# Folding two head pairs of batch 1 as q, then k, in one-bank tiles, with the last 64 queries' scores as a group of their own

## The chip, the core and the metric

The kernel runs on one core of a Trainium2 chip. The metric is the device time of one execution in microseconds (us). The kernel before takes 300.17 us, the median of three runs (299.82 to 300.18).

The engines are named as the profile names them: PE is TensorE's matmuls, PEld its weight loads, DVE is VectorE, ACT is ScalarE, POOL is GpSimd, SP is SyncE, which here only issues transfers. Each engine works through its own list of instructions in the written order and waits, at an instruction, for the results that it needs from others.

## The reference

Causal attention with a window of 64 over 8 batches, 8 heads, 576 positions and head size 64, followed by a two-layer network on all 4608 tokens with the gate h * relu6(h + 3) / 6 between the layers:

```
scores = (q @ k.transpose) / sqrt(64)
rel = pos[:, None] - pos[None, :]
scores = where((rel >= 0) & (rel < 64), scores, -1e9)
attn_out = softmax(scores) @ v                       # (8, 8, 576, 64)
x = attn_out.transpose(0, 2, 1, 3).reshape(4608, 512)
h = x @ w_in                                         # w_in: 512 x 2048
out = (h * clip(h + 3, 0, 6) / 6) @ w_out            # w_out: 2048 x 512
```

## The kernel before, in words

**Two interleaved halves.** The network is cut into nine tiles of 512 tokens. For tile t the hidden layer H(t, fc) is made for 16 blocks fc of 128 features (`s1_part`, L737): four matmuls each, one for each pair of heads, since a pair's two heads of 64 make 128 input rows. ScalarE and VectorE apply the gate (L750, L755) and write `gT`. Then the output rows Y(u) of four blocks of 128 tokens are made (`s2_part`, L776), 16 matmuls each in parts of four, copied out of PSUM (L789) and stored by SP. Batch t + 1's attention is put into the gaps of tile t, for tile t + 1 needs its result. Tile 1 reads the last rows of batch 0 and most of batch 1.

**Attention of one batch.** The eight heads are handled as four pairs, 0 to 3. For each pair there are: the transposed q and k; the scores (L581) of eight blocks of 64 queries with the two blocks of keys that each can see; the exponential (L597, ScalarE) and the multiplication with a mask of zeros and ones (L606, VectorE), which give `pT`; the sums with the values V. The ninth block of 64 queries of all four pairs forms an item of its own, "e", with its own tile `p9`.

**What is special in batch 1.** Its q and k are not turned by a transfer but loaded with nine tokens to a partition into `Aq` and `Ak`, two pairs to a load, and transposed by TensorE (`fold_four`, L540): 36 small transposes for q and 36 for k of two pairs, into one two-bank tile of PSUM each. One copy of 1152 columns for q and one for k (L545) then bring them to `Fq` and `Fk`. The weighted sums of the pairs give rows of queries (`pv_rows`, L626), which VectorE divides by their sums (L636 reciprocal, L637 product); the quotient is transposed back on TensorE (`turn_x`, L652) and copied to `xT` (L368). Only e goes the other way (`pv`, L678): its sums come out transposed already, and the division is made by a logarithm (L684) and an exponential (L687) on ScalarE and a product (L698) on VectorE. All later batches use `pv` for everything.

**V.** Values land as blocks of 128 tokens. Every second block of queries needs keys shifted by 64 tokens, so each pair of heads has two shifted copies of V (`shift_v`, L456): one of 512 elements on 64 partitions and one of 384. A pair's sums need both. For batch 1 each copy may be made by POOL, ACT or DVE, and all need the values landed. In the program before, pair 0's two are made by DVE and ACT, pair 1's by DVE, pairs 2's and 3's by POOL.

**PSUM.** Eight banks: two single ones (`pn`) for the network, and three tiles of two banks, `pb` and two `pa`, which the attention and the hidden layer share.

**What sets the order.** Nothing runs when it can: a planner (`Plan.solve`) gives each operation a cost in ns and places them one by one; for operations with alternatives it picks the engine that would end first by its costs; landing times of POOL's loads are a written list (`NEXT`) with a margin of 300 ns. The order that it finds is then written out, engine by engine, and is fixed. So an edit in one place can change the engine of a copy, the bank of a result and the order of later work. `gate = (hs[4],)` lets batch 1's folds start once H(0, 4) has been placed; which part of the output they stand between, and what comes between two of them, is the planner's doing.

The lines that the change touches, and what leads to them:

Of the kernel before, what the change touches and what calls it, by code (L numbers as in the profile page):

```python
# [222 lines left out]
def kernel(  # L223
# [302 lines left out]
    def fold_four(g0, b, gate, kinds=("b", "a")):  # L526

        pair = slice(g0, g0 + 2)
        names = {n: ("F", n, b, g0) for n in "qk"}
        op = pe(2 * R * 33 + 30, None, [("A", n, g) for n in "qk" for g in (g0, g0 + 1)] + ["fold"], [("ps", x) for x in names.values()],  # L530
                "pick", alloc=tuple(names.values()), kinds=kinds, after=gate, mode="r")

        def em():
            for n, x in names.items():
                to = wide(op, x).bitcast(BF16)
                for j in range(R):
                    for g in (g0, g0 + 1):
                        for h in range(2):
                            r, o = (slice(y * D, (y + 1) * D) for y in (h, home(b, g, h)))
                            nc.tensor.transpose(out=to[o, g - g0, j * D : (j + 1) * D], in_=A[n][r, g, j, :], identity=fold[r, :])  # L540

        op.emit = em

        def ev(eng, n, x):
            cpy(eng)(out=F_[n][:, pair, :].rearrange("d g (p j) -> d g p j", j=R),  # L545
                     in_=wide(op, x).bitcast(BF16)[:, :, 0:S].rearrange("d g (j p) -> d g p j", p=D))

        for n, x in names.items():
            alts = {e: (c, (lambda e=e, n=n, x=x: ev(e, n, x)), False) for e, c in (("DVE", dve(2 * S)), ("ACT", act(2 * S)))}
            e = add("DVE", 0, None, reads=[("ps", x)], writes=[t_key(n, b, g) for g in (g0, g0 + 1)], alts=alts, stream="copy", prio=300)  # L550
            e.frees = (x,)
        return op

    def scores(b, items, gate, stream="att", pr=300, masked=False, kinds=("a",)):

        names = tuple(("S", b, x) for x in items)
# [237 lines left out]

    def attend(b, first, second, stream="att", rows=()):
        a, i0 = scores(b, (0, 1), first, stream)
        z, i1 = scores(b, ("e", 2, 3), second + (a,), stream, kinds=("b", "a"))
        todo = list(zip((0, 1, "e", 2, 3), (*i0, None, *i1)))
        if rows:
            todo.append(todo.pop(2))  # L800
        for x, i in todo:
            if x in rows:
                _, *og = pv_rows(b, x, i, (z,), stream)
                turn_x(b, x, *og, stream, kinds=("b", "a"))
            else:
                pv(b, x, i, (z,), stream)
# [109 lines left out]
    for t in range(NTT):  # L916
        head = HEAD if len(x_parts(t)[1]) == 1 else 0
        if t == 0:
            head = HEAD0
            for gs, n in ((range(2), head), (range(2, NG - 1), SOON)):  # L920
                for fc in range(n):
                    s1_part(t, fc, gs)
        else:
            for fc in range(head):
                s1_part(t, fc, range(NG - 1))

        def seen(t, fc, head):
            return 0 if fc >= head else 2 if t == 0 and fc >= SOON else NG - 1

        hs = [s1_finish(t, fc, s1_part(t, fc, range(seen(t, fc, head), NG))) for fc in range(NFC)]  # L930
        ys = {}
        us = range(4 * t, 4 * t + 4)
        if t == 0:
            for pair in (us[:2], us[2:]):
                for part in (range(0, NFC // 2), range(NFC // 2, 3 * NFC // 4), range(3 * NFC // 4, NFC)):
                    for u in pair:
                        ys[u] = s2_part(u, part)
                for u in pair:
                    s2_close(u, ys[u][-1])
        else:  # L940
            for u in us:
                for cols in (((0, DM),) if u < NT // P - 1 else ((0, 3 * P), (3 * P, DM))):
                    s2_close(u, s2_part(u, range(NFC), cols=cols)[-1], cols)
        b = t + 1
        if b < B:
            if b == 1:
                gate = (hs[4],)
                cast_v(iv, 0, 2, (THREE,) * 3, parts=REST, prio=-2500, pieces=(1,))
                scores(0, ("e",), gate, "pick", kinds=("b", "a"))
                pv(0, "e", None, (), "pick")  # L950
                then(load_vrows(1, NE, chain))
                for g in range(0, NG, 2):
                    fold_four(g, 1, gate)
                for g in range(NG):
                    shift_v(g, g + 1, THREE)
                attend(1, gate, gate, "pick", ROWS)
            else:
                for g in range(0, NG, 2):
                    shift_v(g, g + 2, ("ACT", "DVE") if b == 2 else ("DVE",))
                attend(b, (hs[LATE if b > ROWS_FROM else -1],), (hs[-1],))  # L960
            if b + 1 < B:
                load_rows(b + 1)
# [53 lines left out]
```

## Time and profile before

| | |
|---|---|
| median of three runs | 300.17 us |
| the profiled execution | 299.94 us |
| its span, first to last instruction | 298.2 us |
| granted TensorE clock | 0.999 |
| PE busy | 287.2 us, 96% |
| ACT busy | 206.5 us, 69% |
| DVE busy | 199.8 us, 67% |
| POOL busy | 121.9 us, 41% |
| output matmuls (L776), bank pn, 128x512 | 533 recorded, 124.9 us |
| fold of q, then k, of pairs 2 and 3 | starts at 41.17 and 41.48 us |
| hidden layer of tile 1 | starts at 52.12 us |
| hidden layer of tile 2 | starts at 83.68 us |

A row of the profile in order of time has the start, the duration, the engine, the line of the kernel, the operation, what it writes and reads, the shapes and how many instructions were merged; in brackets is how long the engine stood idle before it and what ended that. Matmuls are pipelined: the next row may start before the one above has ended, and a single record may be missing. A row of grouped instructions ends with the busy time, the mean time of one in ns, and the idle time ahead of them. For transfers, "DMA to landing" counts from the start of the issuing instruction.

### The profile page before, as it was taken

Reading aid. Unit: us, or ns where it says so; the run is one execution under the profiler, and the core shown is the slowest. Engines: PE = TensorE matmul, PEld = TensorE weight load, DVE = VectorE, ACT = ScalarE, POOL = GpSimd, SP = SyncE. Lnnn points to the kernel's source line nnn. Section 1 sums busy time; section 2 is a strip of 40 time slices with the busy share of each in tenths; the row PEclk is TensorE's granted clock in tenths of the full one; section 3 lists DMA queues with packets and bytes.
Section 4 is the critical chain, followed back from the end, with each engine's and each line's share of the span. In section 5 each row is a group of like instructions: output and inputs, shape, how many; then the busy total and the mean of one; then the engine's idle time right before and its main releaser. Section 6 shows DMA issues by size and latency. Waiting matters only on the chain.

```text
span 298.2 us, 6926 instructions
## 1 busy us (share of the span) xinstructions
PE 287.2 (96%) x2780; PEld 153.4 (51%) x2825; DVE 199.8 (67%) x327; ACT 206.5 (69%) x319; POOL 121.9 (41%) x170
## 2 busy tenths in 40 slices
PE   6899998999999999999999999999999999999996
PEld 6544555445544554455687554455445544444443
DVE  4768639777777975878678767878677868106700
ACT  3878636887968795778687958886787768227611
POOL 8884667069547916930992069405000000000000
PEclk9999999999999999999999999999999999999999
DMA  8999999999999999989996899969900110110011
GB/s 187 189 207 206 203 191 176 191 95 151 132 201 150 117 151 196 169 55 209 142 165 40 139 184 171 68 118 167 116 2 35 37 70 1 37 70 35 0 73 70
DMA packets 137680, 36.66 MB, mean 123 GB/s; under 512 B 126256, under 2 KB 132912, under 8 KB 137648
## 3 DMA queue, kind: packets, MB, share of 16 engines
q0 software_dynamic: 98816, 17.80, 73.9%
q1 hardware_dynamic: 38688, 18.12, 25.2%
q8 instruction: 22, 0.36, 0.5%
q10 hardware_dynamic: 144, 0.29, 0.4%
q14 instruction: 10, 0.08, 0.1%
HBM read 36.70 MB, written 9.44 MB: 155 GB/s over the span
## 4 chain that ended last, share of the span: by engine, by line
PE 81%; DMA 10%; POOL 3%; issue 3%; DVE 2%; ACT 0%; POOLq 0%; DVEq 0%
PE pn L776 36%; PE pn L737 16%; PE pa L737 12%; PE pb L737 9%; DMA Aq<-in_q_dram 4%; DMA V<-in_v_dram 4%; PE pa L678 4%; DMA Ak<-in_k_dram 2%; PE pa L581 2%; PE pa L776 1%; PE pb L678 1%; DVE opg L637 1%; DVE pT L606 1%; POOL V L389 0%; POOL Aq L389 0%
## 5 line engine op out<-in xcount | busy, mean ns | idle before, releaser
L776 PE MATMUL pn<-wout,gT 128*128 128x512 bf16 x533 | 124.9, 379 | 2.1 <-issue 1.1
L737 PEld LDWEIGHTS <-win 128*128 128x128 bf16 x640 | 62.0, 98 | 60.5
L776 PEld LDWEIGHTS <-gT 128*128 128x128 bf16 x592 | 54.5, 98 | 58.0 <-issue 0.2
L737 PE MATMUL pn<-xT,win 128*128 128x512 bf16 (+1 forms) x270 | 61.1, 357 | 0.3
L750 ACT ACTIVATE t<-pn,half 128x512 bf16<-128x512 f32 x62 | 42.6, 689 | 8.7 <-PE pn L737 8.3
L755 DVE SCALAR_TENSOR_TENSOR gT<-t,pa 128x512 bf16<-128x512 bf16 x47 | 32.2, 687 | 24.2 <-ACT t L750 23.9
L737 PE MATMUL pa<-xT,win 128*128 128x512 bf16 (+1 forms) x202 | 48.0, 358 | 0.4
L755 DVE SCALAR_TENSOR_TENSOR gT<-t,pn 128x512 bf16<-128x512 bf16 x62 | 42.5, 686 | 8.4 <-ACT t L750 8.1
L389 POOL DMA_DIRECT2D nk<-in_k_dram x55 | 42.0, 797 | 4.8 <-DMA Tk<-nk 4.1
L389 POOL DMA_DIRECT2D V<-in_v_dram x40 | 33.2, 848 | 14.4 <-PE pa L678 12.0
L750 ACT ACTIVATE t<-pa,half 128x512 bf16<-128x512 f32 x47 | 32.2, 686 | 8.9 <-PE pa L737 8.5
L698 DVE TENSOR_TENSOR xT<-pa,rec 64x512 bf16<-64x512 f32 (+1 forms) x48 | 32.0, 667 | 9.3 <-ACT rec L687 8.4
L737 PE MATMUL pb<-xT,win 128*128 128x512 bf16 (+1 forms) x153 | 36.3, 357 | 0.5 <-issue 0.5
L755 DVE SCALAR_TENSOR_TENSOR gT<-t,pb 128x512 bf16<-128x512 bf16 x35 | 24.0, 686 | 16.2 <-ACT t L750 16.1
L789 ACT COPY osb<-pn 128x512 f32<-128x512 f32 x18 | 10.5, 585 | 33.1 <-PE pn L776 33.1
L684 ACT ACTIVATE rec<-pa 64x512 f32<-64x512 f32 (+1 forms) x48 | 27.6, 574 | 5.1 <-PE pa L678 4.0
L750 ACT ACTIVATE t<-pb,half 128x512 bf16<-128x512 f32 x35 | 24.2, 690 | 7.6 <-PE pb L737 7.5
L389 POOL DMA_DIRECT2D nq<-in_q_dram x30 | 27.0, 900 | 3.2 <-DMA wout<-in_moe_w_out_dram 1.6
L597 ACT ACTIVATE pT<-pa 128x1024 bf16<-128x1024 f32 x25 | 24.6, 1021 | 1.0 <-PE pa L581 0.9
L606 DVE TENSOR_TENSOR pT<-pT,mask 128x1024 bf16<-128x1024 bf16 x28 | 19.2, 704 | 3.7 <-ACT pT L597 3.6
L678 PEld LDWEIGHTS <-V 128*128 128x128 bf16 x448 | 16.8, 98 | 6.7 <-DVE xT L698 0.8
L854 POOL COPY scrap<-Tq 128x1 bf16<-128x1 bf16 x5 | 0.9, 189 | 45.3 <-DMA Tq<-nq 45.3
(93 smaller groups left out, 203.9 us busy)
## 6 DMA issues: line engine op xcount, KB each, us to landing
out_dram<-osb SPq DMA_DIRECT2D x35, 256.0 KB, 3.1
V<-in_v_dram POOLq DMA_DIRECT2D x28, 128.0 KB, 5.7
nq<-in_q_dram POOLq DMA_DIRECT2D x24, 128.0 KB, 4.7
nk<-in_k_dram POOLq DMA_DIRECT2D x41, 64.0 KB, 4.0
wout<-in_moe_w_out_dram POOLq DMA_DIRECT2D x4, 512.0 KB, 14.5
win<-in_moe_w_in_dram POOLq DMA_DIRECT2D x3, 512.0 KB, 9.3
V<-in_v_dram POOLq DMA_DIRECT2D x12, 64.0 KB, 6.0
Aq<-in_q_dram POOLq DMA_DIRECT2D x2, 288.0 KB, 13.7
```

What stands on the lines that cost most here:

```text
L389: em = lambda: e.dma_start(out=out_ap, in_=in_ap)
L581: nc.tensor.matmul(to[o, home(b, g, h) if x == "e" else h, y * D : (y + 1) * D], lhsT=w, rhs=q_cols(b, r, g, j), start=not masked, stop=no ...
L597: nc.scalar.activation(out=p_[:].rearrange("p j h c -> p h j c"), in_=wide(add_far if masked else op, name)[:, :, 0 : n * D].rearrange("p ...
L606: nc.vector.tensor_tensor(out=pp, in0=pp, in1=mask[:, m0 : m0 + n, :, :].rearrange("p j h c -> p (j h c)"), op=MULT)
L678: nc.tensor.matmul(wide(op, name)[:, h, y * D : (y + 1) * D], lhsT=V[:, blk, g, h * D : h * D + P], rhs=p_[:, y, home(b, g, h) if end else ...
L684: add("ACT", act(n), lambda h=h: nc.scalar.activation(out=rc[rows[h], 0:n], in_=wide(op, name)[rows[1 - h], h, 0:n], func=LN), reads=[key] ...
L698: nc.vector.tensor_tensor(out=o, in0=a, in1=z, op=MULT)
L737: nc.tensor.matmul(bank(op, name)[:, to : to + n], lhsT=win16[:, g, fc * P : (fc + 1) * P], rhs=xT[:, g, o : o + n], start=(g == 0), stop= ...
L750: nc.scalar.activation(out=t1[ti][:], in_=bank(op, name), func=RELU, bias=half[:], scale=1.0 / 6.0)
L755: nc.vector.scalar_tensor_tensor(out=gT[:, fc, :], in0=t1[ti][:], scalar=1.0, in1=bank(op, name), op0=MIN, op1=MULT)
L776: nc.tensor.matmul(bank(op, name)[:, 0:n], lhsT=gT[:, fc, col : col + P], rhs=wout16[:, fc, js], start=(fc == 0), stop=(fc == NFC - 1))
L789: alts = {e: (f(n), (lambda e=e: cpy(e)(out=osb[oi][:, js], in_=bank(op, name)[:, 0:n])), False) for e, f in (("DVE", dve), ("ACT", act))}
```

## The change: two folds in place of one, and e after pairs 2 and 3

For pairs 2 and 3 of batch 1 `fold_four` is replaced by two calls of a new function `fold_two`, one for q and one for k. Each makes the same 36 transposes, but a pair's go to a tile of its own (one bank of it is used), and each pair has a copy of its own of 576 columns, for which the planner picks the engine. q's fold waits only for q's load, k's only for k's. Pairs 0 and 1 stay with `fold_four`.

In `attend`, batch 1's second group of scores was e, 2, 3 in one operation. Now 2 and 3 are one operation and e another that follows it. No load is changed.

```diff
+    def fold_two(n, g0, b, gate, kinds=("b", "a")):
+        pair = (g0, g0 + 1)
+        names = tuple(("F", n, b, g) for g in pair)
+        op = pe(R * 38 + 30, None, [("A", n, g) for g in pair] + ["fold"], [("ps", x) for x in names], "pick",
+                alloc=names, kinds=kinds, after=gate, mode="r")
+        def em():
+            for j in range(R):
+                for g, x in zip(pair, names):
+                    to = bank(op, x).bitcast(BF16)
+                    for h in range(2):
+                        r, o = (slice(y * D, (y + 1) * D) for y in (h, home(b, g, h)))
+                        nc.tensor.transpose(out=to[o, j * D : (j + 1) * D], in_=A[n][r, g, j, :], identity=fold[r, :])
+        op.emit = em
+        def ev(eng, g, x):
+            cpy(eng)(out=F_[n][:, g, :].rearrange("d (p j) -> d p j", j=R),
+                     in_=bank(op, x).bitcast(BF16)[:, 0:S].rearrange("d (j p) -> d p j", p=D))
+        for g, x in zip(pair, names):
+            alts = {e: (c, (lambda e=e, g=g, x=x: ev(e, g, x)), False) for e, c in (("DVE", dve(S)), ("ACT", act(S) - 30))}
+            e = add("DVE", 0, None, reads=[("ps", x)], writes=[t_key(n, b, g)], alts=alts, stream="copy", prio=300)
+            e.frees = (x,)
+        return op
...
     def attend(b, first, second, stream="att", rows=()):
         a, i0 = scores(b, (0, 1), first, stream)
-        z, i1 = scores(b, ("e", 2, 3), second + (a,), stream, kinds=("b", "a"))
+        if rows:
+            z, i1 = scores(b, (2, 3), second + (a,), stream, kinds=("b", "a"))
+            z, _ = scores(b, ("e",), (z,), stream, kinds=("b", "a"))
+            i1 = (None, *i1)[1:]
+        else:
+            z, i1 = scores(b, ("e", 2, 3), second + (a,), stream, kinds=("b", "a"))
...
                 for g in range(0, NG, 2):
-                    fold_four(g, 1, gate)
+                    if g == 0:
+                        fold_four(g, 1, gate)
+                    else:
+                        for n in "qk":
+                            fold_two(n, g, 1, gate)
```

What the planner makes of it, engine by engine, from q's fold to the hidden layer of tile 1 ("4 Y" are four output matmuls; numbers are pairs):

```
PE before:  4Y 4Y 4Y 4Y 8Y  fold q,k  8Y  scores e,2,3  4Y  sums 0  4Y  sums 1  turn 0  sums 2  4Y  sums 3  turn 1  4Y  turn 2  turn 3  sums e  H
PE after:   4Y 4Y 4Y 4Y  fold q  4Y  fold k  4Y  scores 2,3  scores e  16Y  sums 0,1,2  4Y  turn 0  4Y  turn 1  sums 3  turn 2  sums e  turn 3  H
V copies before:  DVE 0,1,1   ACT 0   POOL 2,2,3,3
V copies after:   POOL 0,0,1   ACT 1,2,3   DVE 2,3
```

One tile later, in the gaps of tile 1's output, the order around batch 2's attention changes too: before, 8 Y stand between its first and second group of scores, and 4, 12, 4 and 16 between its sums and up to tile 2's hidden layer; after, 12 Y, and then 16, 4 and 12. On SP the store of row block 3 moves ahead of the transfer that turns batch 2's q. From tile 2 on the order is the same, with `pa` and `pb` in other turns.

## The prediction

> **What bounds the kernel.** I read the page first, then the instructions in order of time on TensorE, then the other engines in the same stretch.
>
> ```profile
> span 298.2 us, 6926 instructions
> ...
> PE 287.2 (96%) x2780; PEld 153.4 (51%) x2825; DVE 199.8 (67%) x327; ACT 206.5 (69%) x319; POOL 121.9 (41%) x170
> ...
> PE 81%; DMA 10%; POOL 3%; issue 3%; DVE 2%; ACT 0%; POOLq 0%; DVEq 0%
> ```
>
> TensorE is busy 96% of the span and carries 81% of the chain that ended last. A microsecond that it loses anywhere after the start is a microsecond of the total, and one it gains counts only if it is idle there now. All that changes lies between 39 and 52 us (batch 1's attention inside the second product of token tile 0), and, through the planner, in the same place one tile later (66 to 85 us). TensorE there, in order of time (start, duration):
>
> ```profile
> 35.86 5.39 PE L776 MATMUL pn<-wout,gT 128*128 128x512 bf16 x23
> 41.17 0.48 PE L540 MATMUL pb<-fold,Aq 64*64 64x64 bf16 x36
> 41.48 0.50 PE L540 MATMUL pa<-fold,Ak 64*64 64x64 bf16 x36
> 41.91 1.90 PE L776 MATMUL pn<-wout,gT 128*128 128x512 bf16 x7
> 43.74 0.29 PE L581 MATMUL pa<-Fq,Fk 64*128 64x64 bf16 x8
> ...
> 44.43 0.82 PE L776 MATMUL pn<-wout,gT 128*128 128x512 bf16 x3
> 45.71 0.45 PE L626 MATMUL pa<-V,pT 128*64 128x65 bf16 x16 [0.45 <-ACT p L597]
> ...
> 48.22 0.45 PE L626 MATMUL pa<-V,pT 128*64 128x65 bf16 x16 [0.34 <-DVE pT L606]
> ...
> 49.57 0.45 PE L626 MATMUL pa<-V,pT 128*64 128x65 bf16 x16
> 49.97 0.40 PE L652 MATMUL pb<-ident,opg 128*128 128x128 bf16 x4
> ...
> 51.65 0.40 PE L652 MATMUL pb<-ident,opg 128*128 128x128 bf16 x4 [0.19 <-DVE opg L637]
> ...
> 52.12 1.68 PE L737 MATMUL pn<-xT,win 128*128 128x512 bf16 x7
> ```
>
> The waits are 0.45, 0.34 and 0.19 us: 0.98 us is all that this stretch could give back. They come from the engines beside it:
>
> ```profile
> 44.53 0.51 ACT L456 COPY V<-V 64x384 bf16<-64x384 bf16 x1 [1.69 <-DMA V<-in_v_dram]
> 45.06 0.60 ACT L597 ACTIVATE p<-pa 128x512 bf16<-128x512 f32 x1
> ```
>
> ```profile
> 42.04 1.36 DVE L545 COPY Fk<-pa 128x1152 bf16<-128x1152 bf16 x1 [3.65 <-PE pa L540]
> 44.55 1.26 DVE L456 COPY V<-V 64x512 bf16<-64x512 bf16 x3 [1.15 <-DMA V<-in_v_dram]
> 45.85 0.74 DVE L606 TENSOR_TENSOR p<-p,mask 128x512 bf16<-128x512 bf16 x1
> ...
> 50.90 0.69 DVE L637 TENSOR_TENSOR opg<-pa,rsum 128x512 bf16<-128x512 f32 x1
> ```
>
> ```profile
> 44.86 0.91 POOL L389 DMA_DIRECT2D nq<-in_q_dram  x1
> 45.81 2.72 POOL L456 COPY V<-V 64x384 bf16<-64x384 bf16 x4
> ```
>
> Batch 1's values land at 44.5 us; eight shifted copies of V (two for each pair of heads, L456) must follow before a pair's weighted sums (L626) may start. VectorE and ScalarE take theirs the moment the values land; GpSimd takes its four only at 45.81, behind the load that it is still issuing.
>
> **The change, part by part.**
>
> *Folds earlier and split.* q's fold now stands eight output matmuls earlier, k's follows four matmuls after it. A matmul of L776 steps by 0.216 us (24 of them, one record missing, from 35.86 to 41.17 with one change of kind). So q's fold starts at 41.17 - 1.73 = 39.44, k's at 39.44 + 0.43 (41.48 to 41.91, one fold with the change back) + 0.86 + 0.10 = 40.83. Their loads:
>
> ```profile
> 24.64 0.70 POOL L389 DMA_DIRECT2D Aq<-in_q_dram  x1 [2.10 <-DMA win<-in_moe_w_in_dram]
> ...
> 27.17 0.71 POOL L389 DMA_DIRECT2D Ak<-in_k_dram  x1 [1.83 <-DMA wout<-in_moe_w_out_dram]
> ```
>
> ```profile
> DMA to landing us min/median/max: 14.4/14.4/14.4
> ```
>
> ```profile
> DMA to landing us min/median/max: 13.3/13.3/13.3
> ```
>
> q (first line) lands at 39.04, k (second) at 40.47: both just in time, by 0.4 us, so no wait; a late load costs up to 0.4. The 72 transposes stay 72. One more departure from the output matmuls and back costs 0.43 - 0.31 (41.17 to 41.48, a fold alone) = 0.12, and 0.10 to enter: +0.22 us.
>
> *Copies out of the folds.* Two of 1152 columns become four of 576:
>
> ```profile
> L518 DVE COPY Fq<-pn 128x576 bf16<-128x576 bf16 x1 | 0.8, 759 | 0.3 <-PE pn L513 0.3
> ...
> L518 ACT COPY Fk<-pn 128x576 bf16<-128x576 bf16 x2 | 1.3, 645 | 0.0
> ...
> L456 POOL COPY V<-V 64x512 bf16<-64x512 bf16 x3 | 1.9, 646 | 0.1
> L456 POOL COPY V<-V 64x384 bf16<-64x384 bf16 x3 | 1.9, 618 | 0.2
> ```
>
> 0.76 and 0.65 us, side by side. k's copy starts some 0.56 after its fold does (41.48 to 42.04), at 41.39, and ends at 42.15. TensorE has four matmuls in between and comes to the scores at 40.83 + 0.43 + 0.86 + 0.10 = 42.22: a wait of 0 to 0.1, and the scores of pairs 2 and 3 are out 1.5 us sooner than now.
>
> *Scores of the last 64 queries apart.* The same 40 score matmuls, 0.69 us (43.74 to 44.43), with e's eight at the end. Their exponential, 0.60, moves behind those of pairs 2 and 3, so the 0.45 us wait of pair 0's sums for it goes. TensorE then does 16 output matmuls, 42.95 + 3.45, and reaches pair 0's sums at 46.5.
>
> *What is late next: V's copies.* The written order gives them out anew. Because ScalarE has three exponentials and VectorE three masks from 43 to 46 us, pair 0's two copies now go to GpSimd, with one of pair 1's; ScalarE gets three (behind e's exponential), VectorE two (behind the masks). Nothing in the change makes GpSimd free sooner: the load issued at 44.86 holds it to 45.81, as now. Pair 0 is complete at 45.81 + 0.646 + 0.618 = 47.07, pair 1 at 47.69. TensorE runs in order, so pair 0's sums wait from 46.5 to about 47.15, pair 1's start at 47.77, pair 2's at 48.07 (a step of 0.3: 49.57 to 49.97 is 0.40 with a change of kind). Then 0.40 to the output matmuls, 0.96 for four with the change: first transposition 49.43; 0.24; four more; second one 50.63; pair 3's sums 50.96. Its quotient is the next wait: VectorE's reciprocal and product take 0.92 (the product at 50.90 ends at 51.59, its reciprocal began 0.23 before it), so pair 3's transposition starts at 50.96 + 0.45 + 0.92 + 0.12 for two hand-overs = 52.45, against 51.65 now, though e's sums have been moved ahead of it to fill. Hidden layer of tile 1: 52.45 + 0.24 = 52.69 against 52.12: **+0.57 us**. Unknown is what GpSimd's copies take in company; its own four here took 2.72, 0.68 each, and single ones 0.50 to 0.85. At 0.50 the term is +0.2, at 0.85 about +0.95. I take the mean of the rows. Below zero it cannot go while these copies begin at 45.81.
>
> *One tile later.* The new state of the banks lets the planner put twelve instead of eight output matmuls ahead of batch 2's second group of scores; for that only 32 instead of 36 stand between its first sums and the next hidden layer. Now:
>
> ```profile
> 73.67 0.63 PE L678 MATMUL pb<-pT,V 128*128 128x64 bf16 x16
> ...
> 79.75 0.64 PE L678 MATMUL pa<-pT,V 128*128 128x64 bf16 x16
> ...
> 83.68 0.81 PE L737 MATMUL pa<-xT,win 128*128 128x512 bf16 x3
> ...
> 84.97 0.38 PE L737 MATMUL pa<-xT,win 128*128 128x512 bf16 x1
> ```
>
> ```profile
> 74.34 1.20 ACT L684 ACTIVATE rec<-pb 64x512 f32<-64x512 f32 x2 [1.41 <-PE pb L678]
> ```
>
> ```profile
> 83.16 1.39 DVE L698 TENSOR_TENSOR xT<-pa,rec 64x512 bf16<-64x512 f32 x2
> ```
>
> From first sums to hidden layer 10.01 us, and 1.29 more to the first matmul that reads pair 3 (84.97). Pair 3's last product ends at 84.55, 10.88 after the first sums, through ScalarE's row of logarithms and exponentials that starts at 74.34. Slack 0.42. Four matmuls fewer take 0.86: the slack becomes -0.44, and a store's copy that ScalarE now does ahead of this row adds some 0.05: **+0.5 us** (0.3 to 0.6).
>
> *Queues.* GpSimd has three copies instead of four, so its later loads go out 0.6 sooner: nothing waits for them. On SP the store of row block 3 passes ahead of the transposition of q:
>
> ```profile
> 53.17 3.00 SPq L391 DMA_TRANSPOSE Tq<-nq  x1
> 56.28 0.55 SPq L389 DMA_DIRECT2D out_dram<-osb  x1
> ```
>
> Its copy is done by 51.5, so its 0.55 of issue ends before 53.17, and the transposition, which waits for its loads, stays. If it doesn't, 0.55 on a transfer whose readers start at 66 us.
>
> Sum: 0.57 + 0.5 = +1.05 us (the 0.22 for the switches is inside the first term). The profiled execution took 299.94, 0.23 below the median of 300.17; against it 301.0, as a median **301.2 us**.
>
> **Rivals.** (a) *GpSimd's copies are held up by VectorE.* Before, a mask of this shape took 0.74 beside GpSimd's first copy (45.85), and without one
>
> ```profile
> 69.55 0.43 DVE L606 TENSOR_TENSOR p<-p,mask 128x512 bf16<-128x512 bf16 x1 [0.18 <-ACT p L597]
> ```
>
> 0.43: one waits for the other. In the new order VectorE masks without a pause when GpSimd comes to its copies, the last mask about 45.7 to 46.15, so GpSimd would begin 0.34 later: +0.34 and up to 0.2 from longer copies, 301.6 us. Against it: GpSimd may come first, as before. The Trainium skill, "SBUF — State Buffer", section "Who interferes with whom", says that a VectorE instruction with two SBUF inputs and a GpSimd one that reads SBUF exclude each other for the whole instruction, and whichever starts first wins; the 0.74 against 0.43 agrees, and this rule speaks against the change. (b) *V's copies are hidden anyway:* if GpSimd is done with pairs 0 and 1 about 0.6 sooner, only the later tile's 0.5 stays: 300.6 to 300.7, no change. Against it: 45.81 depends on loads that are untouched. (c) *Faster:* the three waits go (0.98), the switch costs 0.22, and the later row of ScalarE finds its slack: 300.17 - 0.76 = 299.4. That needs pair 0's copies by 46.5, so GpSimd free by 45.2, and a row 0.5 shorter than 10.88; nothing in the profile offers either.
>
> **Chances.** Forecast 0.55 (own range 300.9 to 301.5), (a) 0.22, (b) 0.15, (c) 0.08. Within 0.2% (0.6 us), about what a measurement of this kernel can tell from no change, lies only (b); so slower 0.77, same 0.15, faster 0.08. The range 300.5 to 301.9 takes in (b), the forecast and (a) with GpSimd's copies at 0.85.
>
> **What would show it.** q's fold near 39.4, k's near 40.8 without a wait; no wait of pair 0's sums for ScalarE, but one of about 0.6 for GpSimd's V; pair 3's transposition waiting for VectorE at 52.4; hidden layer of tile 1 near 52.7; a wait of 0.5 at its pair 3 one tile later, for VectorE. I am wrong if pair 0's sums start by 46.6, if k's load is late, or if tile 2's hidden layer runs through.

## The result and the profile after

The changed kernel takes 300.88 us (median of 8 executions, 300.47 to 301.22), the kernel before 300.05 (median of 8, 299.70 to 300.63): a ratio of 1.0025, 95% interval 1.0016 to 1.0034, so 0.83 us slower. (Ratios and intervals in this document are those on record; a ratio can differ a little from the quotient of the two medians beside it.) The profiled execution of the changed kernel took 300.65 us, that of the kernel before 299.94.

From the page of the changed kernel: span, busy time by engine, the chain that ended last.

```profile
span 298.9 us, 6935 instructions
...
PE 287.8 (96%) x2780; PEld 153.7 (51%) x2825; DVE 198.4 (66%) x326; ACT 208.4 (70%) x323; POOL 120.7 (40%) x169
...
PE 86%; DVE 3%; issue 3%; POOL 3%; ACT 2%; DMA 2%; DVEq 0%; ACTq 0%; POOLq 0%
```

TensorE has 0.6 us more of busy time for the same 2780 recorded matmuls, and the span is 0.7 us longer. TensorE in order of time, in the changed stretch and then one tile later:

```profile
32.71 0.48 PE L540 MATMUL pa<-fold,Aq 64*64 64x64 bf16 x36
...
39.65 0.22 PE L567 MATMUL pb<-fold,Aq 64*64 64x64 bf16 x2
...
41.02 0.22 PE L567 MATMUL pa<-fold,Ak 64*64 64x64 bf16 x2
...
42.40 0.89 PE L608 MATMUL pa<-Fq,Fk 64*128 64x64 bf16 x32
43.13 0.28 PE L608 MATMUL pb<-Fq,Fk 64*128 64x64 bf16 x8
43.34 3.63 PE L803 MATMUL pn<-wout,gT 128*128 128x512 bf16 x15
46.90 1.16 PE L653 MATMUL pa<-V,pT 128*64 128x65 bf16 x31
...
52.10 0.40 PE L679 MATMUL pa<-ident,opg 128*128 128x128 bf16 x4 [0.41 <-DVE opg L664]
52.33 1.89 PE L764 MATMUL pn<-xT,win 128*128 128x512 bf16 x7
...
74.71 0.63 PE L705 MATMUL pb<-pT,V 128*128 128x64 bf16 x16
...
83.86 0.81 PE L764 MATMUL pa<-xT,win 128*128 128x512 bf16 x3
...
85.66 0.38 PE L764 MATMUL pa<-xT,win 128*128 128x512 bf16 x1 [0.34 <-DVE xT L725]
```

The rows at 39.65 and 41.02 are the first transposes of the two new folds. Three things are to be seen. The first row, the fold of pairs 0 and 1, is ahead of anything that the change touches, and it already stands at 32.71 against 32.47 in the trace of before. Tile 1's hidden layer (52.33) is 0.21 late against 52.12, which is no more than that. The matmul that reads pair 3 one tile later (85.66) is 0.69 late against 84.97, and has the wait of 0.34 for VectorE that was not there. So this one pair of traces puts 0.48 us (0.69 less 0.21) on the later tile and nothing on tile 1. The medians are 0.83 apart, and what lies between is what the experiments had to find.

The engines beside it, in the same two places (VectorE, GpSimd, then ScalarE and VectorE one tile later):

```profile
42.07 0.76 DVE L572 COPY Fk<-pb 128x576 bf16<-128x576 bf16 x1 [1.09 <-PE pb L567]
```

```profile
45.89 1.76 POOL L456 COPY V<-V 64x512 bf16<-64x512 bf16 x3
```

```profile
75.52 1.20 ACT L711 ACTIVATE rec<-pb 64x512 f32<-64x512 f32 x2
...
84.21 1.39 DVE L725 TENSOR_TENSOR xT<-pa,rec 64x512 bf16<-64x512 f32 x2
```

VectorE's copy of pair 3 of k begins at 42.07, though its fold was done at 41.57 (k's fold starts at 41.02): half a microsecond late, and the scores that need it stretch to 0.73 us (42.40 to 43.13). GpSimd's copies of V begin at 45.89, behind its load, and one tile later the last product ends at 85.60, with ScalarE's row starting at 75.52.

### The profile page after: what moved, and what is told of

The parts are those of the page before. It is cut to its first block, busy times and chain, and to the rows that moved or that the text cites. A ratio compares the mean times of both kernels' runs of the same rounds, so it can differ in the third digit from the quotient of the medians.

```text
span 298.9 us, 6935 instructions
## 1 busy us (share of the span) xinstructions
PE 287.8 (96%) x2780; PEld 153.7 (51%) x2825; DVE 198.4 (66%) x326; ACT 208.4 (70%) x323; POOL 120.7 (40%) x169
## 4 chain that ended last, share of the span: by engine, by line
PE 86%; DVE 3%; issue 3%; POOL 3%; ACT 2%; DMA 2%; DVEq 0%; ACTq 0%; POOLq 0%
PE pn L803 36%; PE pn L764 18%; PE pa L764 13%; PE pb L764 10%; PE pa L705 3%; PE pa L608 2%; DMA V<-in_v_dram 2%; DVE xT L725 2%; PE pa L803 1%; ACT rec L711 1%; POOL V L389 1%; DVE opg L664 1%; POOL Ak L389 1%; ACT pT L624 1%; PE pb L705 1%
## 5 line engine op out<-in xcount | busy, mean ns | idle before, releaser
L764 PE MATMUL pa<-xT,win 128*128 128x512 bf16 (+1 forms) x197 | 46.6, 357 | 0.7 <-DVE xT L725 0.3
L782 DVE SCALAR_TENSOR_TENSOR gT<-t,pa 128x512 bf16<-128x512 bf16 x46 | 31.5, 687 | 23.7 <-ACT t L777 23.4
L777 ACT ACTIVATE t<-pa,half 128x512 bf16<-128x512 f32 x46 | 31.5, 687 | 9.3 <-PE pa L764 8.8
L764 PE MATMUL pb<-xT,win 128*128 128x512 bf16 (+1 forms) x157 | 37.3, 357 | 0.5 <-issue 0.5
L782 DVE SCALAR_TENSOR_TENSOR gT<-t,pb 128x512 bf16<-128x512 bf16 x36 | 24.7, 686 | 16.3 <-ACT t L777 16.3
L777 ACT ACTIVATE t<-pb,half 128x512 bf16<-128x512 f32 x36 | 24.9, 690 | 7.7 <-PE pb L764 7.7
L624 ACT ACTIVATE pT<-pa 128x1024 bf16<-128x1024 f32 x26 | 25.6, 1021 | 1.9 <-PE pa L608 1.1
L633 DVE TENSOR_TENSOR pT<-pT,mask 128x1024 bf16<-128x1024 bf16 x28 | 18.8, 689 | 4.7 <-ACT pT L624 4.7
```

What stands on the lines that cost most here:

```text
L624: nc.scalar.activation(out=p_[:].rearrange("p j h c -> p h j c"), in_=wide(add_far if masked else op, name)[:, :, 0 : n * D].rearrange("p ...
L633: nc.vector.tensor_tensor(out=pp, in0=pp, in1=mask[:, m0 : m0 + n, :, :].rearrange("p j h c -> p (j h c)"), op=MULT)
L764: nc.tensor.matmul(bank(op, name)[:, to : to + n], lhsT=win16[:, g, fc * P : (fc + 1) * P], rhs=xT[:, g, o : o + n], start=(g == 0), stop= ...
L777: nc.scalar.activation(out=t1[ti][:], in_=bank(op, name), func=RELU, bias=half[:], scale=1.0 / 6.0)
L782: nc.vector.scalar_tensor_tensor(out=gT[:, fc, :], in0=t1[ti][:], scalar=1.0, in1=bank(op, name), op0=MIN, op1=MULT)
```

## Experiments

A table first, because one trace says little here. From trace to trace the first stage ends up to 1.5 us earlier or later: the fold of pairs 0 and 1 stands between 32.16 and 33.71 us. GpSimd's copies of V, which follow loads, begin between 45.46 and 46.09 in all of them. So tile 1's hidden layer has to be read against the fold of its own execution. The last column but one is the time from there to the hidden layer of tile 3 (two tiles on), which is 62.76 us in the kernel before. What follows, from tile 3's hidden layer to the last instruction, takes 183.33 to 183.35 us in all thirteen traces. So whatever makes one profiled execution longer than another lies ahead of tile 3: in the start of tile 1's hidden layer or in that column.

| kernel | fold | tile 1's hidden layer | from the fold to it | from it to tile 3's | median, us |
|---|---|---|---|---|---|
| before | 32.47 | 52.12 | 19.65 | 62.76 | 300.05 |
| before, more warm-up | 33.44 | 52.27 | 18.83 | 62.76 | 300.13 |
| before, twelve outputs | 33.57 | 52.35 | 18.78 | 63.26 | 300.37 |
| changed | 32.71 | 52.33 | 19.62 | 63.23 | 300.88 |
| changed, again | 33.17 | 52.31 | 19.14 | 63.21 | 300.68 |
| changed, eight outputs | 33.48 | 52.77 | 19.29 | 63.22 | 300.72 |
| the same again | 33.27 | 52.45 | 19.18 | 63.77 | 301.28 (one) |
| eight outputs, shifted | 33.48 | 52.62 | 19.14 | 63.50 | 301.13 |
| eight outputs, more warm-up | 33.71 | 52.85 | 19.14 | 63.08 | 300.88 |
| changed, VectorE's stream | 32.32 | 52.49 | 20.17 | 63.49 | 300.87 |
| changed, pair 0's values | 33.50 | 52.78 | 19.28 | 63.00 | 300.70 |
| folds alone | 32.16 | 51.86 | 19.70 | 63.62 | 300.52 |
| last scores alone | 32.73 | 52.21 | 19.48 | 62.77 | 300.68 |

Beside the changed kernel the kernel before had a median of 300.05 us; beside the changed one again, twelve outputs, eight outputs and pair 0's values also 300.05; beside the shifted one and the two single parts 300.13; beside more warm-up and VectorE's stream 299.95.

**The changed kernel again.** No edit.

> The changed kernel once more, to part what its one profiled execution cannot part. In that trace the fold of pairs 0 and 1 already stands at 32.71 us against 32.47 in the trace of before (+0.24), ahead of anything that the change touches; tile 1's hidden layer starts at 52.33 against 52.12 (+0.21, so about 0 net of that start), and one tile later the matmul of pair 3 at 85.66 against 84.97 (+0.69, so +0.46 net). Theory 1 (only the later wait costs; the early start is chance): the offset at the fold is another one here, between -0.3 and +0.3, and net of it tile 1's hidden layer again stands at 0 +-0.1 and the matmul of pair 3 at +0.45 +-0.1; medians then differ by 0.4 to 0.6 us. Theory 2 (as the prediction had it, tile 1's hidden layer is late by itself and the one trace an exception): the hidden layer net of the offset +0.4 to +0.6, medians +0.8 to +1.1. Theory 3 (the offset belongs to the changed program): the offset at the fold is +0.2 to +0.3 again, medians +0.6 to +0.8. The copy of pair 3 of k on VectorE, 0.48 us late in the first trace (start 42.07, its fold ended about 41.5): late again by 0.4 to 0.6 if it belongs to the order, under 0.1 late if it was chance.

Measured: 300.68 us, ratio 1.0019 (1.0010 to 1.0028). The fold stands at 33.17, tile 1's hidden layer at 52.31: although the stage began 0.46 us later than in the first trace, its end is at the same place. The copy on VectorE is late by half a microsecond again (42.53, its fold started at 41.48). So the offset is none of the program's (theory 3 falls), the late copy is. Theories 1 and 2 are both too simple: what the first stretch costs depends on when it begins, which the other traces settle.

**The later order alone, put into the kernel before.**

```diff
-attend(b, (hs[LATE if b > ROWS_FROM else -1],), (hs[-1],))
+attend(b, (hs[LATE if b > ROWS_FROM else -1],),
+       (hs[-1],) + ((yops[4, 8],) if b == 2 else ()))   # yops[4, 8]: the third stretch of output matmuls
```

> The kernel before with that one order put in: batch 2's second score group behind the third stretch of the output layer (12 output matmuls before it instead of 8); folds, score groups and tile 1's attention as before. Theory 1: a wait of 0.3 to 0.5 us at pair 3 of tile 2's hidden layer, that matmul 0.45 +-0.1 later than in the kernel before, and +0.35 to +0.55 us of time. Rival (the wait needs the change's own tile 1 as well, for instance the later copies of V or other buffers): no wait, time within 0.15 us of the kernel before. If the changed kernel is more than 0.2 us above this one, something else in it costs the difference.

Measured: 300.37 us, ratio 1.0011 (1.0002 to 1.0021), so +0.32. TensorE:

```profile
33.57 0.48 PE L540 MATMUL pa<-fold,Aq 64*64 64x64 bf16 x36
...
52.35 1.68 PE L737 MATMUL pn<-xT,win 128*128 128x512 bf16 x7
...
85.70 0.38 PE L737 MATMUL pa<-xT,win 128*128 128x512 bf16 x1 [0.33 <-DVE xT L698]
```

The wait is there without anything else of the change, and from tile 1's hidden layer to tile 3's it takes 63.26 us, 0.50 more than in the kernel before. Twelve output matmuls ahead of batch 2's second score group are by themselves the later wait. In time the +0.32 is a little under the +0.35 to +0.55 that was expected, with an interval of 0.06 to 0.63. The changed kernel, 300.68 on the same chip, is 0.31 above this one, more than the 0.2 that was set as the mark: something else in it costs the difference. The same rows show the other thing: in the old order a start of the stage that is 1.10 us later (33.57 against 32.47) moves the hidden layer by 0.23 only.

**That order taken out of the changed kernel.**

```diff
-attend(b, (hs[LATE if b > ROWS_FROM else -1],), (hs[-1],))
+z = attend(b, (hs[LATE if b > ROWS_FROM else -1],), (hs[-1],))
+if b == 2:
+    yops[4, 8].follows.add(z)      # second score group before the third stretch again
```

> The changed kernel with one order undone: batch 2's second score group is again ahead of the third stretch of the output layer (8 output matmuls before it as in the kernel before, not 12). Nothing in tile 1's own attention moves. Theory 1 (the later wait is the whole cost): no wait of 0.34 at pair 3 of tile 2's hidden layer, and 0.45 +-0.1 us faster than the changed kernel on the same chip, so between -0.1 and +0.15 against the kernel before. Theory 2 (tile 1's hidden layer late as well): 0.45 faster than the changed kernel, but still +0.3 to +0.6 against the kernel before. Rival: the wait at pair 3 comes from something other than the count of output matmuls (the copies of V, the loads); then the time stays within 0.15 us of the changed kernel's and the wait stays.

Measured: 300.72 us, ratio 1.0021 (1.0010 to 1.0032): nothing gained, although the wait at pair 3 is gone. TensorE stops somewhere else, inside batch 2's second group of scores:

```profile
69.30 0.63 PE L608 MATMUL pa<-Tq,Tk 64*64 64x64 bf16 x53
70.24 0.28 PE L608 MATMUL pa<-Tq,Tk 64*64 64x64 bf16 x11 [0.31 <-issue]
```

Sixty-four equal matmuls, one operation, break off after 53: from the start of one matmul to that of the next it takes 0.50 us, where the others step by 0.01, and "issue" says that the profile shows nothing that was waited for. The rival as I had put it (the wait stays) is wrong, and so is theory 1's gain.

**What that stop is.** Three more kernels with eight outputs. The first is the same program again, the next two change only how many matmuls keep TensorE busy before the first loads (41 in the others), which moves all that follows along its instruction stream.

```diff
-for _ in range(int((op.start - 350) * 0.95 / (IDLE / 1.2))):
+for _ in range(int((op.start - 350) * 0.95 / (IDLE / 1.2)) - 3):    # shifted; "+ 10" in the other
```

> The kernel with eight outputs once more, for its trace alone. If the stop of 0.50 us inside batch 2's second score group belongs to the program (to the place in the stream or to the order), it is there again, at the same matmul (54th of 64 of pairs 2 and 3). If it was chance, it is gone, and from the start of tile 1's hidden layer to that of tile 3's it takes 62.76 us as in the kernel before, not 63.22.

> The kernel with eight outputs again, with three of the matmuls left out that only keep TensorE busy before the first loads (38 instead of 41, in a stretch after which TensorE stands 0.93 us for data anyway). It moves nothing but where TensorE's instructions lie in its stream. In the run with eight outputs the wait at pair 3 was gone, but TensorE stood 0.50 us in the middle of batch 2's second score group (a weight load at 69.73, the next at 70.24) with no semaphore in between, and the time stayed at +0.67 against the kernel before. Theory A (that stop belongs to the place in the instruction stream): it is gone or elsewhere, and the time falls by 0.3 to 0.5 us against the run with eight outputs, to +0.2 to +0.4 against the kernel before. Theory B (chance of one execution): gone here too, but the time as it was, +0.55 to +0.75. Theory C (it belongs to this order of the work): there again, time +0.55 to +0.75.

> The kernel with eight outputs, with ten more of the matmuls that only keep TensorE busy before the first loads (51 instead of 41, some 0.8 us in a stretch that has 0.9 us to spare). It moves nothing but TensorE's place in its instruction stream, by 20 instructions. With eight outputs TensorE stood 0.50, 0.86 and, with seven instructions fewer, 0.60 us inside batch 2's second score group, three matmuls later for the seven instructions, and went on 1.4 to 1.5 us after a 16 KB transfer of the instruction queue ended (68.78, 68.97, 69.03 us; begun at 67.3 to 67.7, when GpSimd's loads fill the transfer engines; in the kernel before begun at 65.31, ended 66.19, and no stop). Theory D (the stop waits for that piece of the instruction stream): asked for 20 instructions earlier, the transfer begins before GpSimd's loads, at 65.5 or earlier, the stop is gone, and the time falls by 0.4 to 0.7 us against the kernels with eight outputs, to +0.15 to +0.4 against the kernel before. Theory C (the stop belongs to the order of the work): it is there, 0.5 to 0.9 us, at the same matmul, time +0.65 to +1.1.

TensorE at that place, in the run again, the shifted one, and the one with ten more:

```profile
68.98 0.63 PE L608 MATMUL pa<-Tq,Tk 64*64 64x64 bf16 x53
70.47 0.28 PE L608 MATMUL pa<-Tq,Tk 64*64 64x64 bf16 x11 [0.86 <-issue]
```

```profile
69.15 0.66 PE L608 MATMUL pa<-Tq,Tk 64*64 64x64 bf16 x56
70.40 0.26 PE L608 MATMUL pa<-Tq,Tk 64*64 64x64 bf16 x8 [0.60 <-issue]
```

```profile
69.38 0.55 PE L608 MATMUL pa<-Tq,Tk 64*64 64x64 bf16 x43
70.11 0.35 PE L608 MATMUL pa<-Tq,Tk 64*64 64x64 bf16 x21 [0.19 <-issue]
```

The same program stops at the same matmul (53 and 11). With three matmuls fewer in front it stops three later (56 and 8), with ten more ten earlier (43 and 21). So the stop belongs to a place in the instruction stream and to no piece of the work. What arrives there is seen in the transfers: the queue named "instruction" moves 16 KB at a time. In the kernel before, the one that matters lies between 65 and 66.3 us; in the run again, between 67 and 69 (packets, MB, share of 16 engines in that window):

```profile
q0 software_dynamic: 1059, 0.13, 163.1%
q8 instruction: 1, 0.02, 4.2%
```

```profile
q0 software_dynamic: 2241, 0.28, 222.1%
q8 instruction: 1, 0.02, 5.2%
```

A share of 4.2% of 16 engines over 1.3 us is 0.88 us, of 5.2% over 2 us 1.65 us. The packets of GpSimd's loads (q0) add up to 163% and 222% of the engines' time in these windows, so they overlap, and the 16 KB transfer runs beside them. Beginning, end of that transfer and the first matmul behind the stop: 67.56, 68.78, 70.24 (eight outputs); 67.32, 68.97, 70.47 (again); 67.68, 69.03, 70.40 (shifted); 66.96, 68.61, 70.11 (more warm-up); and, with the folds alone, 67.23, 68.40, 69.86. TensorE goes on 1.37 to 1.50 us after the transfer ended, in all five traces. What the stop costs is best read from the table: 0.32 to 1.01 us more than 62.76 to tile 3. In the kernel before, the transfer ended at 66.19; 1.5 us on, at 67.69, TensorE was not there yet (these 64 scores start at 68.69). In the changed kernel it ended at 68.15; 1.5 us on is 69.65, and twelve output matmuls instead of eight bring TensorE to the place 0.86 us later, at about 70.2, after that: the order with the wait at pair 3 hides the stop.

My theory D was right on what it is and wrong on the size: ten matmuls more brought the transfer forward by 0.4 to 0.7 us, not past the loads; the stop shrank to 0.4, and the time is 300.88 against 299.95 (1.0027, 1.0017 to 1.0038) instead of the +0.15 to +0.4 that I gave. The shifted kernel has 301.13 against 300.13 (1.0035, 1.0017 to 1.0052): theory A was right that the stop moves with the stream, but the time rose instead of falling to +0.2 to +0.4, for the stop only moved on. Why the transfer begins later with the two-pair folds (66.56 to 68.11 us) than with the old ones (64.92 to 66.33) isn't shown; that GpSimd's loads are in front of it is only what the shares suggest.

The same sign is to be found where the change has no part, in the first stage. In the kernel before, and in the kernel before with ten matmuls more of warm-up (tested below):

```profile
12.16 0.41 PE L513 MATMUL pn<-fold,Aq 64*64 64x64 bf16 x14 [0.19 <-issue]
```

```profile
12.15 0.26 PE L581 MATMUL pa<-Fq,Fk 64*128 64x64 bf16 x6 [0.42 <-issue]
...
18.34 0.59 PE L737 MATMUL pa<-xT,win 128*128 128x512 bf16 x2 [0.51 <-issue]
```

The first of these breaks off a group of 18 after 4, the second a group of 16 after 10, which is ten matmuls ahead in the order of work. TensorE goes on 1.40, 1.41 and 1.49 us after a 16 KB transfer ended (at 10.76, 10.74 and 16.85).

The Trainium skill, "Runtime: NRT & Kernel Launch", section "Instruction fetch mechanics", says that an engine's instructions come in blocks of 16 KiB, 256 instructions each, by a DMA queue of its own while the block before is running, and that the cost of a crossing is mostly hidden. The page of the profile of the kernel before agrees on the size for q8 (0.36 MB in 22 transfers); those of q14 are half as large:

```profile
q8 instruction: 22, 0.36, 0.5%
...
q14 instruction: 10, 0.08, 0.1%
```

Which engine a queue serves, the profile doesn't say; TensorE's 2780 matmuls and 2825 weight loads over 22 transfers are 255 instructions each, which fits q8. Most of the 22 crossings cost nothing here: in the kernel before, the 0.19 us above is the longest idle time of TensorE put down to "issue". The crossing that comes in a run of 64-column matmuls, at 0.01 us each, while GpSimd's loads are under way, costs 0.3 to 1.0 us in the five traces.

**VectorE's late copy.** The same question for the copy of pair 3 of k.

```diff
-nc.vector.memset(mask32[:], 1.0)),
+nc.vector.memset(mask32[:], 1.0),
+*(nc.vector.memset(half[:, 0:1], 0.5) for _ in range(4))),
```

> The changed kernel with four tiny fills more on VectorE in the first microsecond and a half, which move VectorE's instruction stream by four. In every run with the two-pair folds VectorE's copy of pair 3 of k starts 0.48 us after its fold is done, with no wait of its own. It is the 65th instruction of VectorE's main stream. Theory D (it waits for the next piece of VectorE's instruction stream): with four instructions more the late one is another, four instructions ahead of it; the copy starts within 0.1 us of its fold's end, the scores of pairs 2 and 3 follow without the hole of some 0.2 us, and tile 1's hidden layer starts up to 0.2 us earlier at a late start of the stage. Time 0 to 0.2 us below the changed kernel's +0.6 to +0.8. Theory E (the copy is late for what happens beside it, on ScalarE or GpSimd): late by 0.45 to 0.5 us again.

Measured: 300.87 against 299.95 us (1.0027, 1.0015 to 1.0040). VectorE and TensorE:

```profile
41.27 0.76 DVE L572 COPY Fk<-pb 128x576 bf16<-128x576 bf16 x1 [0.69 <-PE pb L567]
```

```profile
42.01 0.64 PE L608 MATMUL pa<-Fq,Fk 64*128 64x64 bf16 x32
42.49 0.28 PE L608 MATMUL pb<-Fq,Fk 64*128 64x64 bf16 x8
...
46.26 0.26 PE L653 MATMUL pa<-V,pT 128*64 128x65 bf16 x4
47.41 0.80 PE L653 MATMUL pa<-V,pT 128*64 128x65 bf16 x27 [0.89 <-POOL V L456]
```

With four instructions more in front the copy starts 0.09 us after the semaphore of its fold (41.18), and the scores take 0.48 instead of 0.73 us. So the lateness belongs to a place in VectorE's stream, as theory D had it, and theory E falls. That the copy waits for a piece of the stream to arrive isn't shown, and one thing speaks against it: in the eight other traces with two-pair folds the copy starts 0.50 to 0.51 us after its fold's semaphore, though that comes anywhere from 41.03 to 42.56 us, and the last 8 KB transfer of q14 before it ended 1.2 to 2.1 us earlier, at no fixed distance. The time, +0.92 us, didn't fall as theory D had said; what the early copy is worth at a late start this trace can't show, for its start was early. The fold stood at 32.32, the earliest but one, and what TensorE saved went into a wait of 0.89 us for GpSimd's second copy of V, which follows the loads. The 64 scores one tile later also took 1.00 us instead of 0.72, with the 16 KB transfer ending at 68.99 and TensorE going on 1.58 later: a small stop for instructions in spite of the twelve outputs, and 63.49 us to tile 3.

**Pair 0's values off GpSimd.**

```diff
-shift_v(g, g + 1, THREE)
+shift_v(g, g + 1, THREE if g else ("ACT", "DVE"), 400 if g == 0 else 0)
```

> The changed kernel with the two shift copies of pair 0's values taken from GpSimd: both are made early on VectorE (about 44.5 us), where VectorE has a hole between the masks; GpSimd keeps copies of later pairs. In the changed kernel the sums of pairs 0 and 1 stop twice for GpSimd's copies, 0.25 + 0.17 = 0.42 us. Theory 1: the sums of pair 0 do not stop, tile 1's hidden layer starts 0.2 to 0.5 us earlier than in the changed kernel (net of the start), the wait of 0.34 one tile later stays, and the time falls by 0.2 to 0.5 us against the changed kernel, to within 0.25 of the kernel before. Rival 1 (TensorE's wait moves on: turn 3 waits for VectorE's quotient in any case, 0.41 us now): hidden layer within 0.1 us of the changed kernel's, no gain, the wait at turn 3 grows to about 0.8. Rival 2 (VectorE, with two copies more, holds up GpSimd's): GpSimd's copies longer than 0.75 us, no gain or a loss.

Measured: 300.70 us, ratio 1.0024 (1.0012 to 1.0036), no gain. TensorE:

```profile
46.01 0.45 PE L653 MATMUL pa<-V,pT 128*64 128x65 bf16 x16
...
52.33 0.40 PE L679 MATMUL pa<-ident,opg 128*128 128x128 bf16 x4
52.78 0.59 PE L764 MATMUL pn<-xT,win 128*128 128x512 bf16 x2
```

Pair 0's sums run through and the last turn waits for nothing, as theory 1 had it; yet the fold is 19.28 us ahead of the hidden layer, not less than the 19.14 of the changed kernel at a like start. At such starts there was no wait for GpSimd left to remove, and what was gained at the last turn was spent ahead of the hidden layer (0.45 from the turn to it instead of 0.23). The wait one tile later is there as expected. Rival 1 is right that TensorE's wait moves on, though not on where. Rival 2 had GpSimd's copies at more than 0.75 us: the first took 0.92, the other three 0.50 to 0.59.

**Each part alone.** Folds in two, with the scores of the last 64 queries left in their group; and the reverse, with `fold_four` for all.

```diff
-z, i1 = scores(b, (2, 3), ...)            # folds alone
-z, _ = scores(b, ("e",), (z,), ...)
+z, i1 = scores(b, ("e", 2, 3), ...)
...
-for n in "qk":                            # last scores alone
-    fold_two(n, g, 1, gate)
+fold_four(g, 1, gate)
```

> One part of the change alone: pairs 2 and 3 of batch 1 folded q, then k, in one-bank tiles; the scores of the last 64 queries stay in one group with those of pairs 2 and 3. One tile later 8 output matmuls stand before the second score group, as in the kernel before. Where tile 1's hidden layer starts is told against the start of tile 0's (the first stage ends between 16.5 and 17.6 us from execution to execution): 35.62 at 16.50 and 34.75 at 17.60 in the old order, 35.59 at 16.74, 35.11 at 17.20 and 35.26 at 17.51 in the changed one. Theory 1 (at late starts the changed order of turns and sums costs 0.4 to 0.5 us because the last turn waits 0.41 us for VectorE's quotient; at early ones 0.2): this order too ends with a turn right behind its sums, so +0.2 to +0.45 us against the kernel before, and no wait at pair 3 one tile later. Rival (the separate score group, not the folds, makes the stage longer): hidden layer at start + 34.8 or at 52.1, whichever is later, and a time within 0.15 us of the kernel before.

> The other part alone: scores of the last 64 queries as a group of their own behind those of pairs 2 and 3, with the folds of both pairs together as in the kernel before. One tile later 8 output matmuls before the second score group. Theory 1: the sums of the last 64 queries and a turn come last here as well, the last turn waits 0.3 to 0.5 us for VectorE's quotient, and the hidden layer starts 0.3 to 0.7 us later than in the kernel before at the same start; no wait at pair 3 one tile later; +0.3 to +0.7 us. Rival (the folds make the stage longer): time within 0.15 us of the kernel before.

Measured: folds alone 300.52 against 300.13 us (1.0011, 0.9995 to 1.0026), last scores alone 300.68 (1.0009, 0.9993 to 1.0024). Neither can be told from no change with certainty. TensorE in the first, and in the second:

```profile
46.40 0.38 PE L653 MATMUL pa<-V,pT 128*64 128x65 bf16 x12 [0.49 <-POOL V L456]
...
51.86 0.81 PE L764 MATMUL pn<-xT,win 128*128 128x512 bf16 x3
...
69.86 0.28 PE L608 MATMUL pa<-Tq,Tk 64*64 64x64 bf16 x11 [0.79 <-issue]
```

```profile
51.98 0.40 PE L679 MATMUL pa<-ident,opg 128*128 128x128 bf16 x4 [0.53 <-DVE opg L664]
52.21 1.89 PE L764 MATMUL pn<-xT,win 128*128 128x512 bf16 x8
```

Both have eight outputs and no wait at pair 3. The folds alone get the stop for instructions in its place (63.62 us to tile 3). They also reach the hidden layer at 51.86, earlier than any other kernel, from the earliest start; so the 52.1 that the rival set as the earliest start is not a fixed bound for this order. The last scores alone show the wait for the quotient that theory 1 named, 0.53 us, and run through afterwards (62.77); but that profiled execution took 300.02, 0.66 under its own median, and what the others paid isn't in its trace.

**The kernel before with more warm-up.** The same "+ 10" as above, in the kernel before.

> The kernel before with the same ten matmuls more ahead of the first loads, so that it too asks for its instructions earlier. If some executions of the kernel before (299.4 to 300.8 us) stop for instructions, the median falls by 0.1 to 0.4 us; if none does, it stays within 0.1 us. Its trace is also another look at tile 1's stage in the old order: from the fold of pairs 0 and 1 to the hidden layer 19.65 us where the fold stands at 32.47, 18.78 where it stands at 33.57; between them for a start between, with the hidden layer never before 52.1.

Measured: 300.13 against 299.95 us (1.0003, 0.9994 to 1.0012), the same: the shift gains nothing here. It doesn't show that the kernel before never stops for instructions, since the trace of this run has the two stops of 0.42 and 0.51 us shown above. They lie ahead of the fold, and a late start costs the old order little. TensorE:

```profile
33.44 0.48 PE L540 MATMUL pa<-fold,Aq 64*64 64x64 bf16 x36
...
52.27 1.68 PE L737 MATMUL pn<-xT,win 128*128 128x512 bf16 x7
```

18.83 us, beside 18.78 in the other late start of the old order, so that line holds. No kernel tried is faster than the one before.

## Why the prediction was right

The direction, the two places and most of the size held: +1.05 us was forecast against the profiled execution, +0.83 and +0.63 came out in the two comparisons. The absolute forecast, 301.2, is 0.3 to 0.5 too high: 0.12 of that because the median of three runs it started from, 300.17, stood above that of eight, 300.05, and the rest in the first term. The later term is shown by an experiment that puts it in alone. The first is read from the traces, and what it is made of is in part argued.

- *One tile later, +0.5 (0.3 to 0.6).* Right. +0.47 and +0.45 in two traces of the changed kernel (63.23 and 63.21 against 62.76), +0.50 when that order alone is put into the kernel before. Place, cause (twelve output matmuls ahead of the score group) and the wait for VectorE at pair 3 are as written. The steps hold too: the last product ends 10.89 us after the first sums (74.71 to 85.60), 10.88 before, and the hidden layer starts 9.15 after them, 10.01 less 0.86. Only the 0.05 for the store's copy isn't seen. What I did not see is that the old order with eight isn't free to be had back: with the two-pair folds it runs into the stop for instructions, 0.3 to 1.0 us.
- *Hidden layer of tile 1, +0.57.* Mechanism half right, size too large. What failed is the step "TensorE ... reaches pair 0's sums at 46.5": it took the start of the stage from one execution, whose fold stood at 32.47, nearly the earliest of thirteen (the median is 33.27). At such a start GpSimd's copies do hold the sums up, from 45.89 for 1.76 us, but the first four matmuls run before the second copy is needed, and the end is 0.2 us late (52.33 against 52.12; 0.37 in the trace with VectorE's stream shifted, where GpSimd began at 46.09). In the changed kernel's trace pair 2's sums start at 47.92 (forecast 48.07), the first transposition at 49.14 (49.43), the second at 50.23 (50.63), and the last at 52.10 (52.45): 0.15 us came from the copies and the sums ahead of them, and 0.25 from the two steps behind, sized too long by 0.14 and 0.11; 0.05 was lost again ahead of the last one. At the usual start TensorE comes to the sums at 47.4 to 47.9, behind pair 0's copies, and waits 0.15 us for GpSimd at most. There the old order takes 18.8 us and the new one 19.14, +0.35. Of waits the new order has 0.42 at the last turn, which the term had named ("Its quotient is the next wait"), and 0.25 in the scores for VectorE's late copy, which nothing in the profile announced; the old one has 0.19 to 0.23. Their difference, 0.45, is about that +0.35; the rest isn't worked out. So at a usual start the wait for GpSimd, on which the term stood, is nearly absent, and 0.25 of what stands in its place was not foreseen: that the term came out with the right sign there is in part luck.
- *The two together.* 0.35 + 0.46 = 0.81 at a usual start, 0.2 + 0.46 = 0.66 at an early one. The medians gave 0.83 and 0.63, with intervals of 0.48 to 1.02 and 0.30 to 0.84 us, so they agree with both and can't tell them apart.
- *Folds just in time.* Right. 39.65 and 41.02, less the 0.24 of that execution 39.41 and 40.78, forecast 39.44 and 40.83, with no wait for a load.
- *Copies out of the folds, a wait of 0 to 0.1.* Too small: it was 0.25, for VectorE's copy started half a microsecond after its fold in every trace with two-pair folds but the one with its stream shifted.
- *Queues.* Right: nothing waited for SP or for GpSimd's later loads, the first of which went out at 47.60 instead of 48.48, 0.88 sooner where 0.6 was said.
- *Rivals.* (a), GpSimd's copies held up by VectorE, is seen in part and costs nothing. Three copies took 1.76 us in the first trace of the changed kernel, where VectorE stood idle from 46.8 on, 1.79 in its second and 2.22 in the latest start, in both of which VectorE worked on without a pause; there TensorE came later still. VectorE was held up as well: its last mask took 0.42 us when it started ahead of GpSimd's copies (45.43) and 0.83 beside them (45.89 in the second trace). (b), the copies hidden anyway, is what the traces with a usual or late start show, though for another reason than it gave: GpSimd was no sooner done, TensorE came later. Its 300.6 to 300.7 lies nearer to both medians, 300.88 and 300.68, than the forecast's 301.2; what it lacked is the wait for the quotient. (c) did not come.

## What to carry to other kernels

A profile is one execution. Where some engines follow loads that keep their time and another follows a stage that ends up to 1.5 us earlier or later, a wait in the trace may be missing in most runs; compare several traces by the time from a mark ahead of the change, and work the sum out for the usual start. If a run of equal matmuls breaks off with no releaser, shift the instruction stream by a few instructions: if the break moves along by as many, it belongs to a place in the stream. Whether it waits for instructions to arrive is then read from the transfers of the instruction queue: the restart has to keep a fixed distance from the end of one.

## What was not expected of the hardware

- TensorE stood inside one group of small matmuls in five traces, at a cost of 0.3 to 1.0 us, and went on 1.37 to 1.50 us after a 16 KB transfer of the instruction queue ended; the place moved by 3 and by 10 matmuls with 3 fewer and 10 more in front. Three stops in the first stage, in the old order, keep the same distance.
- VectorE began one copy 0.50 us after the semaphore that released it in eight traces with the two-pair folds, and 0.09 after it when four tiny instructions more stood in front. The delay was the same wherever the copy fell in time; what it is stays open.
- In the old order a start of the stage that came 1.10 us later made the next tile 0.23 us late.
